# Values of one head pair beside the scores of the next in TensorE's order, the values' sum in another PSUM bank, and the third unit's raw keys asked for later

## The chip, the cores and the metric

One Trainium2 chip, one of its cores. The metric is device time in microseconds (us) of one launch. The kernel before takes 630.86 us (median of three runs, 630.76 to 632.21). A core has TensorE (PE in the rows; its weight loads are PEld), VectorE (DVE), ScalarE (ACT), GpSimd (POOL), SyncE (SP, here only a queue that issues DMAs), and 16 DMA engines. Each engine takes its instructions strictly in the order in which the program lists them.

## What is computed

Two stages, in fp32 accuracy. q, k, v are (4 batches, 8 heads, 768 tokens, 64).

```python
k_sum = k.reshape(B, H, 24, 32, D).max(axis=3)          # 24 summary keys
v_sum = v.reshape(B, H, 24, 32, D).mean(axis=3)
scores = concat(where(|i-j| < 16, q k^T / 8, -1e9), q k_sum^T / 8 + log(32))
a = exp(scores - max); a = a / (sum(a) + 1e-9)
attn = a @ concat(v, v_sum)                              # heads side by side: x is (3072, 512)
h = x @ w_in                                             # 512 -> 2048
g = where(h >= 1, h, where(h <= -1, 0, (h + 1)**2 / 4))
out = g @ w_out                                          # 2048 -> 512
```

## The kernel before

The 3072 tokens are cut into seven units, numbered c = 0 to 6 (`BLOCKS`, line 41): four of 384 tokens, three of 512. The change's own words count them from one, so its "unit 3" is c = 2. Within a unit attention runs by head pairs p = 0 to 3, two heads side by side on 128 partitions. While TensorE does the feed-forward of unit c, the attention of unit c + 1 is put between its matmuls, a pair at a time.

Everything is placed by hand. Two long texts, `OPENING` (line 49) and `REST` (line 72), list the steps of the whole program in one order; `do` (line 740) runs through them, and each engine's instruction stream is this order restricted to that engine. A step is a letter and its arguments in hexadecimal: `s21` is the scores of unit 2, pair 1. The letters that matter here:

- `s` (`scores_of_pair`): 24 matmuls (32 in the wide units) of 64 rows by 64 columns, into two PSUM banks `s_ps`. Then `n` (mask, DVE, two instructions, which empty those banks), `i` (row maxima, DVE), `g` (exponentials, ACT), `h` (reciprocals, DVE), `l` (normalising, POOL), `t` (transposes in blocks, DVE, 10 or 12 a pair) into the one tile `turned_blocks`, and `p`.
- `p` (`values_of_pair`, line 553): 24 or 32 matmuls of 128 rows by 64 columns, which multiply `turned_blocks` with the values into one PSUM bank `o_ps`. `X` (ACT, for the wide units ACT or DVE in turn) and for the narrow units `L` (DVE) bring it to SBUF.
- `F` (`ff1`, three matmuls of 384 columns, line 571; four such steps make one `h`), `G H I` (the gate, on ACT, ACT and DVE), `J O` (its high and low parts, ACT and POOL), `B` (`ff2`, line 695: nine matmuls for a narrow unit). From unit 4 the first product is done by seven half products `1` (line 594) with combinations `9`, and the second is `(`, three matmuls a step.
- `r` asks SP for a pair's raw keys, `R` takes their block maxima (DVE, line 352), `C` copies these beside the window keys (POOL, line 357). `y` asks for raw values, `v` for windowed values, `q` and `k` for queries and window keys, `w` fetches weights, `&` writes weight sets back, `o` stores results: all are DMAs on SP's one queue, in the order of the text, and one that waits for its buffer holds up those behind it.

After the opening, PSUM's eight banks are three pools: `ps_h` (two banks: `h`, half products), `ps_acc` (four banks: `acc`, three or four of them held through a unit's whole second product) and `ps_att` (two banks: `s_ps`, `o_ps` and some half products). As the two `s_ps` need both banks of `ps_att` and `o_ps` needs one, `s` of a pair stands in the order somewhat behind `p` of the pair ahead of it, with some `F` or `B` between.

In SBUF, the tag `"v"` of the pool `load` has two buffers, which windowed values of units 0 and 1 share with the raw keys and raw values of all units from 2 on (lines 131, 163, 169). In the opening the raw keys `r20` and `r21` are asked for between the windowed values `v10`, `v11`, `v13`, `v12` of unit 1, and `R20`, `R21`, `C200` stand near the opening's end. The weights come as raw words, which ACT (lines 237, 243), DVE (250, 255) and POOL (265, 269) turn into two fp32r halves during the opening; `w` steps 14 and 15 are the last two fetches.

Of the kernel before, what the change touches and what calls it, by code (L numbers as in the profile page):

```python
# [74 lines left out]
l201 l200 H16 o01 &10 o02 z21 B12 %001 %000 J13 O13 G14 I16 t202 t20a %014 t205 y22 r22 F150 H14 t209 %002 t207 t200
t206 F151 v20 &61 B13 C210 %015 I14 t208 F170 F171 F152 J16 %016 J14 x200 %017 F153 %003 t204 t20b t203 t201 %004 O14
O16 G15 p20 H15 X20 &05 q22 %005 R22 %006 L20 u22 I15 B14 &01 s21 J15 F172 %007 n211 v21 n210 y23 &02 r23 F173 G17
%101 F180 F181 i21 H17 I17 &51 &11 &03 %100 k22 q23 &04 F182 %102 g213 %103 z22 g212 g211 g215 g214 g210 F183 O15 %104
G18 h21 H18 F190 I18 %105 u23 l210 l211 F191 x210 t216 F192 t215 F193 B15 t219 t21b t214 t210 t212 t211 t217 F1a0 F1a1
J17 F1a2 B16 F1a3 %106 O17 %107 t213 G19 &12 t218 %110 H19 J18 t21a B17 O18 p21 %111 I19 &13 %112 G1a H1a &50 I1a %113  # L80
F1c0 F1c1 X21 C220 L21 F1c2 %114 s22 %115 F1b0 F1b1 %116 n220 n221 %200 i22 J19 %117 %201 g224 F1b2 g223 g225 g220 B18
O19 F1c3 R23 J1a O1a %202 z23 g222 F1b3 g221 %203 h22 G1c %204 H1c G1b I1c v22 &15 k23 l220 l221 H1b %205 B19 I1b %206
F1d0 x220 %207 J1b F1d1 F1d2 F1d3 F1f0 F1f1 O1b t220 t228 t224 t223 G1d F1f2 &14 H1d t222 t225 t221 t22b t227 B1a %210
C230 t229 t22a %211 t226 p22 J1c X22 I1d F1e0 y40 &20 &23 %212 O1c %213 F1e1 L22 F1e2 %214 %215 s23 %301 n231 n230 i23
F1e3 %216 F1f3 G1e B1b %300 H1e g234 g231 v23 &22 g233 J1d I1e %302 F200 %217 g232 %303 &24 k30 g230 O1d %304 g235
F201 G1f H1f %305 x230 F202 h23 B1c %306 J1e &25 &31 l231 l230 I1f %307 O1e t233 t235 t230 t234 F210 %311 q30 %310
F211 &33 B1d J1f B1e t23a t23b t232 t236 t239 t238 t231 O1f t237 p23 X23 u40 %312 %313 L23 B1f F203 C300 U10 G20 s30
F212 %314 H20 %315 o10 %316 n301 F213 G21 I20 J20 n300 H21 F230 F231 F232 i30 g302 g301 I21 %317 r40 k31 v30 &35 J21
g300 U11 g303 g305 g304 O20 F233 F220 G23 F221 F222 F223 O21 G22 H23 B20 o11 h30 l301 l300 x300 C310 H22 I23 %401 I22
t300 t30a F240 F250 F241 F251 F242 t309 t306 t30b %400 t307 t301 t302 &32 t308 U12 J22 B21 t304 t303 t305 J23 p30 F243  # L90
X30 %402 O22 F252 %403 G24 %404 q31 r41 L30 H24 %405 &34 F253 O23 q40 G25 %406 s31 I24 %407 B22 F260 o12 H25 n310 n311
i31 %411 %410 g311 g315 J24 g314 g313 F261 R41 I25 F262 g312 g310 O24 F263 %412 F270 F271 F272 %413 v31 q32 &42 G26
h31 F273 B23 %414 l310 l311 x310 H26 I26 %415 %416 %417 F280 t316 t314 &43 k32 J26 F281 O26 F282 t31b F283 B24 t31a
t313 G27 H27 J25 t311 t312 t319 t310 t317 t315 t318 %501 %500 I27 &71 &45 y41 p31 %502 X31 %503 L31 F290 O25 C320 G28
%504 %505 F291 H28 F292 %506 s32 B25 J27 n320 n321 i32 F293 %510 %507 g324 I28 g321 g320 g322 g323 g325 O27 B26 v32
&44 %511 u41 R40 F2a0 %512 &52 F2a1 h32 J28 G29 k33 x320 &53 q33 F2a2 %513 l320 l321 H29 %514 I29 %515 F2a3 B27 F2b0
O28 %516 F2b1 G2a J29 H2a F2b2 %517 t32b O29 %600 F2b3 %601 t32a C330 t325 t323 t324 t328 t322 B28 t326 G2b t320 t329
t327 t321 p32 I2a y43 &70 &60 &54 %602 H2b I2b &55 F2d0 J2a X32 F2d1 %603 F2c0 L32 s33 %604 F2c1 %605 %610 %611 n330
n331 %606 %607 O2a i33 F2c2 u43 %612 F2c3 F2d2 F2d3 B29 B2a g331 g334 g335 g330 g333 g332 G2c %613 h33 l331 H2c l330
# [722 lines left out]
```

## Time and profile before

| | |
|---|---|
| median of three runs | 630.86 us |
| profiled execution, its own time | 630.26 us |
| its span, first to last instruction | 628.5 us |
| TensorE busy | 609.4 us, 97% |
| DVE, POOL, ACT busy | 437.9, 393.7, 365.0 us |
| mean rate of DMA | 195 GB/s |

The 1.76 us between span and time lie around the instructions. TensorE's busy time counts modelled ends of pipelined matmuls; how much time a group of matmuls takes is better read from the chain of work that ended last, where each piece lasts until the next begins. In a timeline, the bracket behind a row is the idle time of that engine before it, and what ended it.

### The profile page before, as it was taken

What the parts mean: (1) busy time and instruction counts of PE and PEld (TensorE: products, weight loads), DVE (VectorE), ACT (ScalarE), POOL (GpSimd) and SP (SyncE); (2) the same over time, 40 slices, a digit from 0 to 9 for tenths busy, and PEclk for the clock granted to TensorE, in tenths of its full rate; (3) what the DMA queues carried; (4) which work ended last, traced back from release to release, by engine and by line L of the source; (5) the groups of instructions that cost most, each with busy time, mean ns of one, the idle gap of its engine ahead of it and who ended that gap; (6) DMA issues with size and microseconds to landing.
All of it is one profiled execution on the core that took longest, in us unless ns stands there. A gap on an engine that the chain in (4) does not pass through costs nothing.

```text
span 628.5 us, 12987 instructions
## 1 busy us (share of the span) xinstructions
PE 609.4 (97%) x4628; PEld 535.5 (85%) x4628; DVE 437.9 (70%) x1012; ACT 365.0 (58%) x977; POOL 393.7 (63%) x450
## 2 busy tenths in 40 slices
PE   8689998999999999999999999999999999999996
PEld 7578887788888888898888988879988898989895
DVE  5879785568887789778676788865777765444342
ACT  2779997456454655565465665537556365553542
POOL 2578997655676677663477865669674568735421
PEclk9879999999999999999999999999999999999998
DMA  8989835476554667355678497767696485676521
GB/s 305 329 238 382 269 100 142 140 275 202 155 157 159 171 169 216 103 141 133 178 216 270 116 304 231 196 197 217 184 302 175 124 269 146 175 225 186 172 64 67
DMA packets 85041, 122.56 MB, mean 195 GB/s; under 512 B 27377, under 2 KB 56305, under 8 KB 84977
## 3 DMA queue, kind: packets, MB, share of 16 engines
q1 hardware_dynamic: 71152, 77.68, 40.6%
q0 software_dynamic: 13824, 44.05, 23.9%
q8 instruction: 37, 0.61, 0.4%
q14 instruction: 28, 0.22, 0.1%
HBM read 100.73 MB, written 20.97 MB: 194 GB/s over the span
## 4 chain that ended last, share of the span: by engine, by line
PE 89%; DVE 3%; DMA 2%; ACT 2%; POOL 2%; issue 2%; SPq 0%; POOLq 0%; ACTq 0%; DVEq 0%
PE acc L695 41%; PE h L571 20%; PE h L594 19%; PE o_ps L559 3%; PE s_ps L510 3%; DMA halves<-sets 1%; PE o_ps L449 1%; PE t_ps L437 1%; DMA first<-in_kT 1%; PE s_ps L403 1%; ACT raw L237 1%; DVE den L416 1%; PE h_idle L650 0%; DVE vs L361 0%; DVE e L410 0%
## 5 line engine op out<-in xcount | busy, mean ns | idle before, releaser
L695 PE MATMUL acc<-halves,ghi 128*128 128x512 f32 x720 | 224.2, 393 | 0.0
L682 POOL TENSOR_TENSOR glo<-t,ghi 128x384 fp32r<-128x384 f32 (+1 forms) x112 | 126.9, 1135 | 108.6 <-ACT ghi L677 98.9
L695 PEld LDWEIGHTS acc<-halves,ghi 128*128 128x128 f32 x720 | 135.5, 188 | 24.5
L571 PE MATMUL h<-x,halves 128*128 128x384 f32 x720 | 140.5, 342 | 3.1 <-POOL halves L269 2.2
L695 PE MATMUL acc<-halves,glo 128*128 128x512 f32 x360 | 143.0, 397 | 0.0
L594 PEld LDWEIGHTS h<-halves,halves 128*128 128x128 f32 x1008 | 132.4, 190 | 9.6 <-issue 1.8
L664 ACT ACTIVATE t<-h,ones_half 128x256 f32<-128x256 f32 (+1 forms) x160 | 80.2, 513 | 101.0 <-DVE h L607 56.7
L594 PE MATMUL h<-halves,halves 128*128 128x256 f32 x1008 | 135.7, 283 | 1.0 <-DMA halves<-sets 1.0
L571 PEld LDWEIGHTS h<-x,halves 128*128 128x128 f32 x720 | 125.1, 188 | 11.1 <-POOL halves L269 3.1
L672 DVE SCALAR_TENSOR_TENSOR t<-h,t 128x256 f32<-128x256 f32 (+1 forms) x160 | 73.6, 472 | 48.4 <-ACT t L668 44.2
L550 DVE STREAM_TRANSPOSE turned_blocks<-e 32x256 f32<-32x256 f32 (+1 forms) x240 | 98.4, 410 | 5.8 <-POOL e L538 1.8
L677 ACT CAST ghi<-t 128x384 fp32r<-128x384 f32 (+1 forms) x112 | 61.9, 556 | 60.3 <-PE acc L695 38.6
L695 PEld LDWEIGHTS acc<-halves,glo 128*128 128x128 f32 x360 | 67.8, 188 | 12.0 <-issue 1.3
L580 POOL DMA_DIRECT2D halves<-sets x96 | 53.1, 556 | 31.8 <-PE h L594 30.6
L668 ACT ACTIVATE t<-t 128x256 f32<-128x256 f32 (+1 forms) x160 | 71.0, 458 | 2.9
L528 ACT ACTIVATE e<-e,den 128x120 f32<-128x120 f32 x144 | 55.0, 383 | 18.6 <-DVE den L524 18.4
L607 DVE TENSOR_TENSOR sums_so_far<-h,sums_so_far 128x256 f32<-128x256 f32 x72 | 29.5, 421 | 34.2 <-PE h L594 29.0
L607 DVE TENSOR_TENSOR h<-h,sums_so_far 128x256 f32<-128x256 f32 x96 | 39.0, 426 | 20.2 <-PE h L594 18.8
L538 POOL TENSOR_TENSOR e<-e,den 128x480 f32<-128x480 f32 (+1 forms) x40 | 35.6, 910 | 26.3 <-DVE den L533 12.1
L269 POOL TENSOR_TENSOR halves<-w,halves 128x1024 fp32r<-128x1024 f32 x15 | 36.1, 2409 | 5.7 <-DMA q<-in_q 4.2
L517 DVE SCALAR_TENSOR_TENSOR e<-s_ps,mask_sb 128x480 f32<-128x480 f32 (+1 forms) x40 | 22.8, 602 | 14.0 <-PE s_ps L510 14.0
L630 POOL TENSOR_TENSOR merged<-merged,high_of_sums 128x512 fp32r<-128x512 f32 x16 | 20.7, 1296 | 17.8 <-ACT high_of_sums L628 17.6
(115 smaller groups left out, 688.7 us busy)
## 6 DMA issues: line engine op xcount, KB each, us to landing
halves<-sets POOLq DMA_DIRECT2D x72, 512.0 KB, 4.8
raw<-in_w_in SPq DMA_DIRECT2D x15, 512.0 KB, 10.3
raw<-in_w_out SPq DMA_DIRECT2D x15, 512.0 KB, 9.6
v<-in_vwin SPq DMA_DIRECT2D x22, 288.0 KB, 4.0
out<-o SPq DMA_DIRECT2D x24, 256.0 KB, 3.8
halves<-sets POOLq DMA_DIRECT2D x24, 256.0 KB, 4.3
kraw<-in_kT SPq DMA_DIRECT2D x13, 384.0 KB, 4.3
vraw<-in_vT SPq DMA_DIRECT2D x13, 384.0 KB, 4.3
```

The source lines that it names most:

```text
L528: nc.scalar.activation(out=e, in_=e, func=AF.Exp, bias=dens[c, p][:, 0, u:u + 1], scale=1.0, accum_out=dens[c, p][:, 1, u:u + 1])
L550: nc.vector.transpose(out=turned_blocks[kb * SB:(kb + 1) * SB, :2 * nt, qb * SB:(qb + 1) * SB], in_=e[qb * SB:(qb + 1) * SB, :, at:at + SB])
L571: nc.tensor.matmul(hs[c, f][:, :w], weight["win", f][:, part, k * P:(k + 1) * P], x, start=(k == 0 and n == 0), stop=(k == NK - 1 and n == 2))
L580: nc.gpsimd.dma_start(out=at[:, 0] if n == 3 else at.rearrange("p h n -> p (h n)"), in_=cols)
L594: nc.tensor.matmul(hs[c, q, n][:, :HALF], weights[:, wp, kk], x[:, xp, kk], start=(kk == 0 and m == 0), stop=(kk == 1 and m == 2))
L607: nc.vector.tensor_tensor(out=of if to is None else so_far[:, to], in0=of, in1=so_far[:, so], op=ALU.add)
L664: nc.scalar.activation(out=t, in_=h, func=AF.Relu, bias=ones_half, scale=0.5)
L668: nc.scalar.square(out=t, in_=t)
L672: nc.vector.scalar_tensor_tensor(out=t, in0=h, scalar=1.0, in1=t, op0=ALU.max, op1=ALU.min)
L677: nc.scalar.copy(out=hi, in_=ts[c, f])
L682: nc.gpsimd.tensor_tensor(out=lo, in0=ts[c, f], in1=hi.bitcast(F32), op=ALU.subtract)
L695: nc.tensor.matmul(acc[c, i], a[:, rows], weight["wout", f][:, part], start=(f == first and n == 0), stop=(f == last and n == 2))
```

## The change

One line of code moves `o_ps` out of `ps_att`: into `ps_acc` for units 2 to 4, into `ps_h` for units 5 and 6.

```diff
     def values_of_pair(c, p):
         nt = WIDTH[c] // P
-        o_pss[c, p] = ps_att.tile([P, 512], F32, tag="att", name=f"o_ps{c}_{p}")
+        where, tag = (ps_acc, "ps") if c <= CLASSIC else (ps_h, "h")
+        o_pss[c, p] = where.tile([P, 512], F32, tag=tag, name=f"o_ps{c}_{p}")
```

The order of the opening loses five steps (`r20`, `r21`, `R20`, `R21`, `C200`) and is otherwise the same; the order of the rest is written anew, with these five at its head and `y20`, `y21` behind `r20`, `r21`. Of the many lines these are the ones that the prediction speaks of:

```diff
 OPENING = """
...
-c83 F081 I06 F082 F083 bb1 J07 r20 bb0 F0a0 O07 v11 J06 F0a1 ab q13 F0a2 F0a3 c82 E110 cb0 O06 cb2 cb1 d8 E111 e8 cb3
+c83 F081 I06 F082 F083 bb1 J07 bb0 F0a0 O07 v11 J06 F0a1 ab q13 F0a2 F0a3 c82 E110 cb0 O06 cb2 cb1 d8 E111 e8 cb3 D111
...
-P120 N131 T130 A12 X12 I0f T131 P131 L12 F100 J0f P130 B0d O0e R21 ef O0f A13 X13 F112 L13 C200 F101 F102 F113 F103
...
+T130 A12 X12 I0f T131 P131 L12 F100 J0f P130 B0d O0e ef O0f A13 X13 F112 L13 F101 F102 F113 F103 B0e G11 G10 H10 H11
...
 REST = """
-y21 U01 U00 U02 F130 y20 &41 &30 k21 &21 &40 o00 %011 s20 F131 &00 u20 G12 %010 F132 F133 n201 H12 I12 n200 G13 F140
+&50 &40 U02 F130 U00 r20 r21 F131 G12 F132 H12 R20 y20 R21 C200 U01 y21 o01 I12 s20 F160 F133 n200 %011 F161 %010 F162
...
+&20 t230 x230 t232 t231 J1f t234 &33 t23b B1e t23a t235 L22 O1f B1f %310 %311 C300 %312 p23 X23 s30 %313 U10 %314 %315
+L23 F202 n300 F203 %316 G20 F210 n301 i30 H20 %317 g300 F211 F212 k31 o10 I20 g304 F213 G21 H21 g303 g302 J20 I21 g305
...
+1413 I401 H420 9412 I420 9414 (413 (412 U31 9415 {430 {422 p50 J40 s51 O40 X50 n511 G431 n510 1416 9417 i51 (411 (402
```

TensorE's attention steps in their order, before and after; a plus joins two with no other matmul between:

```
before: s20 p20 s21 p21 s22 p22 s23 p23 s30 p30 s31 p31 s32 p32 s33 p33 s40 p40 s41 p41
        s42 s43 p42 p43 s50 p50 s51 s52 p51 p52 s53 p53 s60 p60 s61 p61 s62 p62 s63 p63
after:  s20 s21+p20 s22+p21 s23+p22 p23+s30 s31+p30 s32+p31 s33+p32 s40+p33 s41+p40 s42+p41
        s43+p42 p43+s50 p50+s51 s52+p51 p52+s53 p53+s60 s61+p60 p61+s62 s63+p62 p63
```

## Rows read from the trace of the kernel before

**Rows 1.** Busy time by stage: window, engines' busy us, clock, DMA share, GB/s.
```profile
98.00:119.00 21.00, 17.97 (x133) 15.38 (x132) 11.52 (x24) 12.46 (x30) 15.27 (x17) 1.00 0.45 122
119.00:345.00 226.00, 225.94 (x1674) 196.96 (x1671) 172.94 (x395) 124.23 (x343) 138.86 (x163) 1.00 0.62 184
345.00:613.00 268.00, 267.04 (x2041) 238.31 (x2040) 172.96 (x423) 147.40 (x412) 167.29 (x200) 1.00 0.66 193
```

**Rows 2.** Chain that ended last, separate visits: start us, us, what.
```profile
128.72 0.78 PE s_ps L510 x24
...
158.73 1.58 PE h L571 x9
160.31 2.08 PE acc L695 x9
...
164.99 0.85 PE o_ps L559 x24
165.84 1.79 PE h L571 x9
167.63 0.78 PE s_ps L510 x24
168.41 1.79 PE h L571 x9
...
304.01 0.98 PE s_ps L510 x32
```

**Rows 3.** Chain that ended last, in the opening: scores and values adjacent.
```profile
94.33 0.78 PE s_ps L403 x24
95.11 0.85 PE o_ps L449 x24
95.96 2.28 PE acc L695 x9
```

**Rows 4.** Timeline of TensorE, late opening: its idle times.
```profile
108.44 2.34 PE L571 MATMUL h<-x,halves_win 128*128 128x384 f32 x12 [1.58 <-DVE t L672]
111.66 0.55 PE L437 MATMUL t_ps<-ident_sb,e 128*120 128x128 f32 x3 [0.88 <-DVE w L255]
...
113.83 0.54 PE L437 MATMUL t_ps<-ident_sb,e 128*120 128x128 f32 x3 [0.57 <-POOL e L432]
```

**Rows 5.** Timeline of ACT, late opening: the wait for the last weights.
```profile
103.96 1.15 ACT L237 ACTIVATE raw<-raw 128x1024 f32<-128x1024 f32 x1 [2.93 <-DMA raw<-in_w_out]
```

**Rows 6.** Timeline of SP, the DMA queue, in the opening.
```profile
69.35 1.09 SPq L292 DMA_DIRECT2D kraw<-in_kT  x1
85.00 0.33 SPq L337 DMA_DIRECT2D v<-in_vwin  x1
...
96.05 0.33 SPq L337 DMA_DIRECT2D v<-in_vwin  x1
96.83 1.06 SPq L228 DMA_DIRECT2D raw<-in_w_out  x2
```

**Rows 7.** Timeline of POOL, late opening and behind it.
```profile
105.55 1.29 POOL L269 TENSOR_TENSOR halves_win<-w,halves_win 128x512 fp32r<-128x512 f32 x1
110.24 1.01 POOL L682 TENSOR_TENSOR glo<-t,ghi 128x384 fp32r<-128x384 f32 x1 [3.40 <-ACT ghi L677]
...
112.99 1.54 POOL L432 TENSOR_TENSOR e<-e,den 128x360 f32<-128x360 f32 x2
...
119.89 0.30 POOL L357 COPY k<-ks 128x144 f32<-128x144 f32 x1
...
128.64 0.20 POOL L757 MEMSET sums<- 128x128 f32 x1
```

**Rows 8.** Timeline of DVE, late opening: the block maxima.
```profile
101.35 0.92 DVE L352 TENSOR_REDUCE ks<-kraw 128x24 f32<-128x768 f32 x1
```

**Rows 9.** Groups by line: the copies that empty a wide o_ps.
```profile
L457 DVE COPY xraw<-o_ps 128x512 f32<-128x512 f32 x6 | 4.1, 690 | 5.5 <-PE o_ps L559 5.5
...
L457 ACT COPY xraw<-o_ps 128x512 f32<-128x512 f32 x6 | 3.5, 580 | 5.9 <-PE o_ps L559 5.9
```

More of the change, by code (lines that the diff above doesn't have):

```diff
@@ new lines @@
+G08 B06 N111 H08 db I08 aa S12 W10 M121 ba1 M120 J08 ba0 G0a we f121 ca1 B07 eb F090 F091 ca0 F092 F093 ca3 H0a ca2
+D110 A10 E121 O08 T111 I0a da ac P111 v13 bc1 B08 G09 X10 cc1 F0c0 ea bc0 H09 cc3 F0c1 ad I09 J09 J0a N110 wf cc0 f120
+bd0 F0c2 F0b0 O09 cc2 dc F0b1 bd1 cd0 O0a cd2 C13 F0b2 L10 cd1 F0c3 W11 F0b3 B09 T110 E120 D121 cd3 G0c G0b P110 H0b
+S13 A11 dd H0c B0a ec M130 I0b q21 ed I0c F0d0 D120 k20 ae F0d1 F0e0 F0e1 J0c F0e2 v12 F0d2 M131 J0b f130 be0 f131 ce0
+N120 O0c be1 E130 ce2 O0b af D130 F0d3 X11 N121 ce1 F0e3 ce3 B0b L11 E131 G0d H0d I0d B0c bf1 de ee cf1 bf0 G0e H0e
@@ L75 @@
[L75 to L99, printed above, removed]
@@ L120 @@
-p50 I401 {423 R51 H420 I420 9414 C511 X50 (413 1416 J40 9417 9415 s51 O40 n510 G421 (412 U31 1415 n511 9416 (411 G431
-H421 G430 H431 {430 {433 {432 x510 (400 (401 1424 k52 {431 v52 o32 i51 C520 H430 I431 I430 I421 g512 g516 g510 1422
-R52 1423 9421 J43 g514 1425 9424 9422 g517 g511 9426 g515 g513 9425 h51 (402 1426 O43 z51 (403 1421 G450 H450 G451
-H451 J42 l511 l510 I450 I451 9423 9427 t519 t518 t511 t515 t510 t513 t51a t516 O42 {443 x511 G440 H440 G441 (432 (430
-(431 (433 1430 I440 J45 q53 o31 t512 t514 t517 9430 H441 O45 t51b (422 y53 C521 {442 {440 (421 (420 (423 1432 9431
@@ new lines @@
+F163 B10 n201 k21 i20 B11 u20 G13 g205 g201 g203 H13 g202 u21 %012 J12 I13 %013 O12 g204 g200 F140 F141 %014 J13 h20
+G16 F142 F143 %015 B12 H16 z20 l201 l200 %016 &10 o00 t207 t200 t202 I16 O13 F170 J16 %017 o02 y22 &01 O16 %001 %000
+&04 v20 G14 F171 F172 t208 H14 u22 t206 I14 t204 F173 t20b t203 %002 t201 B13 J14 G17 &05 q22 t209 t20a F150 F151 %003
+C210 t205 F152 F153 s21 O14 x200 %004 %005 H17 I17 G15 p20 n211 n210 F180 H15 &31 r23 %101 %006 i21 F181 k22 B14 I15
+X20 %007 g213 g211 %100 g210 g215 J15 g212 g214 %102 z21 F182 F183 F190 O15 F191 %103 &02 R23 G18 H18 F192 h21 F193
@@ new lines @@
+F230 F231 U11 F232 O20 &35 y43 F233 F220 F221 F222 J21 g301 O21 G23 F223 h30 H23 G22 l301 l300 I23 H22 B20 I22 U12 &11
+&32 o11 v30 J22 O22 t304 t301 F240 F241 F250 F251 C310 F252 F253 F242 F243 B21 t302 t300 t307 t303 t305 t309 t306 t30b
+t30a G25 J23 H25 t308 %400 %401 %402 %403 %404 %405 x300 O23 s31 %406 G24 p30 B22 n311 n310 i31 H24 I25 I24 &34 o12
+&61 %410 %407 %411 g310 g313 F260 g315 %412 %413 J24 g311 g314 F270 F261 F271 F272 %414 F262 k32 g312 v31 h31 O24 F273
+F263 R41 %415 %416 l311 l310 t315 B23 C320 %417 t31b G26 X30 H26 J25 t317 &43 q32 t312 t319 I26 t310 t311 t316 t31a
@@ new lines @@
+t313 t314 &71 B24 %500 t318 &45 F280 F281 %501 O25 J26 G27 H27 x310 %502 F282 O26 F283 L30 s32 %503 G28 p31 n320 n321
+i32 B25 I27 F290 H28 %504 F291 I28 F292 F293 F2a0 F2a1 %505 g324 g323 J27 %510 %511 g322 &42 r40 g325 %506 q33 k33
+F2a2 g320 v32 &44 O27 g321 G29 X31 F2a3 &52 %507 R40 %512 H29 &53 h32 %513 %514 B26 %515 I29 F2b0 l320 F2b1 l321 %516
+&54 J28 t32a F2b2 t324 t322 t327 L31 t321 t329 x320 t325 C330 O28 G2a t326 H2a I2a t320 t323 t328 F2b3 B27 F2d0 J29
+%517 %601 %600 F2d1 F2d2 %602 O29 &55 y41 t32b G2b F2d3 %603 s33 p32 %604 %605 v33 k40 H2b %606 %607 %611 n331 I2b
@@ new lines @@
+n330 B28 i33 F2c0 g330 g335 z40 %610 &63 q41 &62 g333 g334 g332 J2a F2c1 u41 F2c2 B29 X32 O2a g331 J2b G2d F2c3 O2b
+h33 %612 B2a H2d I2d l331 C400 F2e0 l330 %700 %701 x330 G2c L32 %613 F2e1 H2c I2c F2e2 J2c q40 F2f0 F2f1 F2e3 t331
+t333 F2f2 F2f3 B2b t339 O2c G2e H2e t335 J2d t33b t330 %614 t336 t334 r42 &60 t33a %702 t338 t332 %615 t337 %703 %704
+O2d B2c s40 I2e %705 p33 G2f n401 n400 F310 i40 J2e %706 X33 %616 F311 %707 H2f g404 %617 F312 B2d O2e g405 I2f F300
+g401 g400 g402 g406 u43 L33 g403 J2f g407 F313 F301 O2f F302 h40 R42 G31 l401 l400 H31 F303 G30 B2e I31 F320 H30 &64
@@ new lines @@
+k41 F321 I30 F330 t402 F322 &65 v40 t40b t406 t407 t40a t409 t405 t408 t401 t403 t400 F323 F331 F332 B2f J31 x400 F333
+r43 J30 C410 t404 O31 O30 &73 y42 G32 H32 U20 G33 U21 s41 o21 q43 H33 I32 p40 n410 n411 %711 %710 F340 I33 i41 X40
+g416 g415 g413 g411 g414 z41 u42 F341 F342 F343 F350 %712 F351 B30 g417 g410 F352 J32 g412 F353 B31 O32 G34 h41 R43
+%713 l411 l410 o20 H34 B32 &72 k42 v41 y50 J33 I34 J34 q42 O33 F360 F361 G35 F362 H35 U22 t41b t415 t410 B33 t418 x410
+t414 C420 t416 t417 I35 %714 t413 t412 t41a F370 J35 F371 F372 O34 F363 t419 F373 O35 r50 t411 s42 p41 G36 H36 %715
@@ new lines @@
+F3d1 F3d2 I3c t435 t436 t43b F3d3 G3d F3e0 H3d t439 B3a t437 J3c F3e1 {412 x430 C501 t438 t431 t430 t433 t434 O3c t43a
+t432 F3e2 X42 F3e3 B3b I3d p43 &75 x500 s50 G3e {413 H3e J3d F3f0 I3e X43 O3d n501 ^41 z50 n500 F3f1 <41 q51 r51 ^42
+F3f2 1400 F3f3 B3c >41 i50 1401 <44 <42 9400 G3f g502 g500 H3f >42 v51 k51 J3e g503 g504 g507 g501 I3f u51 >44 O3e
+C510 1403 1402 {420 9401 1404 ^43 9403 B3d g505 G400 g506 R51 h50 <45 H400 9402 I400 9404 l501 l500 1410 J3f <46 1411
+B3e >45 9410 O3f 9405 t505 t503 t50b G411 1412 t507 9413 t501 1405 9406 t500 9411 H411 G410 H410 I411 B3f I410 >46
@@ new lines @@
+t515 t510 t512 t51a t516 C521 {443 O45 x511 t519 9430 (423 v52 (421 x520 {440 t517 t511 t51b I440 t518 t514 (452 1432
+9431 s52 I441 n521 n520 J44 p51 i52 1434 1433 g520 g526 g521 g524 1431 g523 g527 g522 q53 k53 9432 1435 X51 g525 9433
+9434 9436 z52 G460 9435 h52 O44 (442 (453 {451 {441 l520 l521 (451 1436 G470 G471 H471 (450 (443 (441 9437 H470 H460
+I471 I470 (440 I460 1441 1440 t528 t52b t521 t525 t529 J47 G461 9440 1444 t527 {452 v53 t526 t520 r53 H461 O47 (471
+1442 (472 I461 t522 t523 t524 9441 9443 9442 t52a (473 (470 1443 J46 G480 H480 x530 {450 x521 O46 C530 R53 {453 (463
@@ new lines @@
+p52 I480 9444 X52 u53 {460 C531 {463 s53 1446 (460 9445 n531 G491 H491 1445 9447 (462 G481 ^50 {462 {461 n530 H481
+I491 9446 G490 I481 1450 (461 1452 i53 J48 9450 H490 v60 k60 I490 1453 9451 z53 1454 g536 g530 9454 9452 1456 O48 1455
+9455 9457 J49 g531 9456 O49 g533 q60 g537 {471 g534 g532 g535 (493 1451 (492 (490 (483 (491 G4b1 (481 (482 h53 9453
+G4b0 G4a1 H4b1 (480 H4a1 I4b1 1460 H4b0 I4a1 I4b0 G4a0 J4b l531 l530 {470 x531 o30 t536 1463 t539 t537 t533 t530 1464
+t53a 9460 t535 1462 t538 t534 t531 t532 t53b O4b C600 {472 {473 x600 {503 H4a0 (4b0 (4b2 9461 p53 I4a0 9464 9462 s60
@@ new lines @@
+9465 X53 n600 n601 J4a G4d1 (4b3 1470 H4d1 <50 1465 O4a 9466 I4d1 G4d0 1461 ^51 ^52 9463 (4b1 H4d0 1466 i60 I4d0 9470
+G4c0 H4c0 9467 J4d (4a3 1472 1471 g606 G4c1 v61 o31 q61 9471 <51 I4c0 (4a1 (4a0 g605 1474 (4a2 1473 <52 H4c1 g603 <54
+g600 I4c1 9474 9472 k61 {501 J4c {500 >50 {502 O4d {510 >51 ^53 O4c (4d3 (4d2 1475 (4d1 (4c2 1476 9475 9473 g607 g601
+g602 9476 g604 h60 <53 G4e0 G4f1 9477 G4f0 H4f1 (4d0 (4c0 I4f1 H4f0 G4e1 H4e1 H4e0 >52 l601 l600 1500 I4e1 9500 <56
+(4c3 1502 t609 I4e0 I4f0 9501 t606 <55 >54 1504 (4c1 t607 9502 J4e J4f t605 >53 >55 t602 O4f 1503 {511 1510 1505 9504
@@ new lines @@
+t603 9506 {512 9505 t604 1501 G510 (4f0 H510 G511 C610 {513 O4e (4f2 I510 t60b t600 H511 (4f3 1511 (4f1 t608 >56 9503
+I511 (4e1 9510 (4e3 U41 J51 G500 1506 (4e2 (4e0 H500 9513 t60a O51 I500 9507 1512 (510 G501 G520 {520 {521 {522 H501
+H520 t601 I501 1514 9511 I520 9512 1513 9514 s61 9515 n610 n611 U40 o41 J50 i61 O50 x610 U42 G531 p60 (512 (513 H531
+X60 g612 (503 g614 g617 o40 {523 I531 q62 U43 {533 (500 1516 1515 1520 g610 g611 g613 g616 g615 9516 9517 9520 G521
+G530 (511 H530 1521 h61 1522 H521 (502 9523 I530 9521 I521 J53 l611 l610 t617 t610 q63 (501 1526 1524 1523 O53 k62
@@ new lines @@
+{530 v62 t614 t618 9522 t615 (530 o42 o43 (532 (531 G540 t61a {542 J52 t619 t612 9524 9527 1525 {531 O52 (520 (533
+(522 (521 C620 {540 {532 t613 9526 (523 G541 H541 G550 H550 t61b 9525 t611 t616 H540 G551 I541 I540 I550 H551 p61 s62
+k63 J54 I551 X61 1533 1530 J55 n620 n621 O55 9530 (550 1534 1531 1532 i62 O54 {543 {541 {553 9531 9533 g621 g620 (553
+9532 g623 g627 9534 (551 1536 g625 g622 9535 1535 9537 G560 g624 g626 G571 h62 H571 9536 H560 G570 G561 l620 {551 H561
+l621 H570 I571 I560 I561 (543 (541 t62b I570 t626 t62a (552 t628 t622 t620 t623 1540 (540 (542 v63 1541 9540 J57 J56
@@ new lines @@
+1543 C630 O57 O56 1542 {550 1544 (570 (572 9541 9544 t621 {552 9543 t627 9542 t625 9545 1546 (573 (560 (562 (571 G580
+H580 {562 ^60 I580 {563 x620 (563 (561 {560 9547 t629 t624 G591 H591 G581 s63 H581 I581 p62 n631 I591 n630 1545 X62
+J58 9546 i63 1550 G590 1552 9550 H590 1554 9551 I590 9552 1553 1551 g633 J59 1556 1555 O58 {561 O59 9553 9554 9555
+9556 g637 g630 g631 g635 g632 (591 (593 (590 g634 9557 G5b1 G5b0 g636 H5b0 G5a0 I5b0 {572 {573 G5a1 h63 H5a0 H5b1 {570
+{571 x630 H5a1 l631 l630 I5b1 (580 (592 (581 I5a0 (582 I5a1 1560 1562 9560 J5a (583 t633 t639 1564 J5b 1563 t636 9561
@@ new lines @@
+t634 t63a 9562 1565 1566 O5b t63b 9564 9565 9566 t630 G5d1 9567 t631 G5d0 H5d1 {602 O5a I5d1 H5d0 G5c1 (5b2 1561 I5d0
+(5b1 t635 H5c1 (5b0 (5a2 1573 I5c1 t632 9563 (5b3 1570 (5a0 {600 {601 {603 t637 <63 G5c0 H5c0 t638 {613 >63 J5d O5d
+9570 (5a1 p63 (5d2 (5d0 (5a3 X63 I5c0 <60 (5d3 1572 9571 1574 1575 9572 9574 >60 ^62 J5c <62 9576 1576 G5f0 ^61 1571
+O5c 9575 9577 H5f0 (5d1 {611 {612 {610 >62 (5c1 (5c3 G5f1 I5f0 9573 <61 G5e1 H5f1 G5e0 H5e1 I5f1 I5e1 J5f H5e0 >61
+(5c0 1600 (5c2 O5f 1603 I5e0 9600 J5e 1602 O5e <64 ^63 (5f1 (5f2 (5f0 1601 <66 (5e1 (5f3 9601 9603 >64 G600 1604 H600
@@ new lines @@
+J64 {641 {640 O64 9630 1636 (652 9631 (650 (653 1633 9632 (640 1631 9634 9637 9633 {652 9635 (642 (651 1635 G661 9636
+H661 G660 H660 G671 H671 G670 I661 H670 I660 I671 I670 J66 (641 (643 1640 1642 9640 9641 1646 1644 1643 1645 9642 9646
+9644 J67 9647 9645 {653 {650 {651 O66 O67 G681 G691 H691 (673 (670 (672 G690 H681 o52 o53 (663 (671 1641 I681 {660
+9643 I691 {661 {662 H690 G680 I690 (661 (662 (660 1650 J69 9650 H680 1653 1654 O69 I680 (692 1652 9651 (690 1655 9652
+9654 9655 9656 {663 J68 G6b1 G6b0 H6b1 H6b0 (691 1651 (693 1656 I6b1 I6b0 9653 9657 1660 J6b O68 {673 9660 G6a1 {670
@@ new lines @@
+(682 O6b {672 H6a1 (683 G6a0 H6a0 (681 I6a0 I6a1 (680 1664 (6b2 (6b0 1662 (6b1 1663 9661 9664 J6a 9662 9665 G6d1 (6b3
+O6a H6d1 {671 I6d1 (6a3 1665 1666 (6a1 1661 (6a0 9667 9666 9663 G6d0 (6a2 H6d0 I6d0 G6c1 1670 1674 J6d H6c1 9670 G6c0
+I6c1 1672 9671 9672 H6c0 O6d 1673 9674 I6c0 (6d1 1675 9675 (6d3 1676 J6c G6f1 1671 (6d2 (6d0 O6c 9676 G6f0 H6f1 H6f0
+I6f1 9677 9673 G6e1 I6f0 G6e0 J6f H6e0 (6c2 H6e1 O6f (6c0 (6c3 (6c1 (6f0 I6e1 I6e0 J6e O6e (6f1 (6f3 (6f2 (6e2 (6e0
+(6e1 (6e3 U62 U60 U61 U63 o62 o63 o61 o60
```

101 lines of the change are left out of this document (24 added, 77 removed).

## The prediction

> **What bounds the kernel now.** First the busy time by stage [rows 1]. From 119 to 345 us TensorE is busy 225.94 of 226 us, from 345 to 613 us 267.04 of 268: there TensorE is the bound, no other engine comes near, and a change pays only by what it takes from TensorE's own instruction stream. From 98 to 119 us, late in the opening, 3.03 of 21 us are idle: there something else is the bound. So I read two things: in the chain what a visit to the attention costs TensorE, and in the timelines of the late opening who makes it wait.
>
> *A visit.* In the chain nine `h` matmuls take 1.58 us when they follow the feed-forward's own work and 1.79 behind `o_ps`, and again 1.79 behind `s_ps` [rows 2]. So coming back from a visit costs 0.21 us beyond the visit's own 0.85 or 0.78. (The chain books it on the piece behind; I use it only as a price per visit.) The opening holds one place where `s_ps` and `o_ps` of two pairs stand side by side: they take 0.78 and 0.85 as when apart, and the nine `acc` matmuls behind take 2.28 [rows 3] against 2.08 undisturbed [rows 2]. Two visits in one thus pay one return of 0.20, not two.
>
> *The late opening.* TensorE stands idle 1.58, 0.88 and 0.57 us, together the 3.03 [rows 4]. The first two hang on ACT by way of DVE (gate, weight conversion), the third on POOL, whose `glo` had waited 3.40 us for ACT [rows 7]. ACT itself stood for 2.93 us until the last weights landed, at 103.96 [rows 5]. They came late because SP asked for them at 96.83, and SP was late because the windowed values ahead on its queue found no buffer: the raw keys `r20` took one of the two `"v"` buffers at 69.35, so `v11` waited until 85.00 and `v13` until 96.05, with the weights behind [rows 6].
>
> **The change, part by part.**
>
> *Joints.* The new order joins 19 pairs of visits and leaves two single; before, none of 40 was joined. 19 x 0.20 = 3.8 us less, all of it on TensorE's stream where that is the bound [rows 1]. Thirteen joints are scores and then values, as in rows 3. Six are values and then scores, which no row shows: at best they save half as much again (0.3 us, an estimate from that 0.20), at worst they cost another 0.2, if the two shapes disturb each other. I take 0.20, the value of the nearest row; the bounds put the term between -4.4 and -1.4.
>
> A joint goes from tiles of 64 x 64 to tiles of 128 x 64. Rows 3 show that this leaves the pieces at 0.78 and 0.85, and one return of 0.20 behind. The Trainium skill, TensorEngine Tiling (Array Packing), section Tiling Modes, Key Properties, says that a change of tiling mode, not only of tile, drains the TensorE; read strictly, a joint pays a drain of its own. If that cost as much as a return, the 3.8 would vanish; by the row the run-out of the scores is within their 0.78 already, joined or not, and the saving stands. The measurement decides here.
>
> *The opening's DMAs.* Without `r20`, `v11` takes the free buffer at about 69.4, `v13` takes the one that `v11` gets now, at 85.00, and the last weights follow as they now follow `v13`, 0.78 behind: about 85.8 in place of 96.83. From that issue they took some 6 to 7 us to ACT; they lie there by 93, and ACT wants them at 101.03. Its 2.93 us go. Then: the first idle time (1.58) waits for a gate that comes 2.93 earlier; what is late next is `halves_win`, which POOL ends at 105.55 + 1.29 = 106.84 [rows 7], and TensorE was ready at 108.44 - 1.58 = 106.86, so nothing is left of it. The second (0.88) hangs on ACT's conversions, 2.93 earlier against 2.46 wanted: gone. The third wants 3.03 and POOL's chain gains at most 2.93: 0.1 stays. `R20`, 0.92 us of DVE in the midst of it [rows 8], goes too and helps the conversions. So up to 2.9; the ends are 0 (another wait stands right behind) and 3.03 (all the idle time). I take 2.5, near the upper end as each step of it has its row, less something for waits under these that no row shows.
>
> *What moves behind the opening.* `R20`, `R21` and `r20`, `r21`, `y20`, `y21` are now late, not gone. DVE has room: 172.94 us in 226. `C200` goes on POOL from 119.89 to behind the memset that ends at 128.64 + 0.20, so `s20` can have its keys at 128.84 + 0.30 = 129.14 at the earliest [rows 7]. It starts now at 128.72 and stands two `F` steps later in the new order, 2 x 0.53 (a third of 1.58), at 129.8 [rows 2]: 0.6 us of room. All of this shifts together with the opening. I cost it at 0; if `R21` or a `y` holds DVE or SP, up to 0.9 (one block maximum).
>
> *Time to work.* Counted in `F` (0.53), `B` (2.08) and visits, TensorE's work between scores and values of a pair was at least 12.2 us in the order before and is at least 14.4 now: DVE, ACT and POOL get more time for a pair, not less. At the units' ends it is tighter: `F203` needs `X23` and `L23`, at most 0.58 + 0.69 (the wide copies, rows 9, as a bound for the narrow), and has `s30` and `F202` in front, 0.78 + 0.53 = 1.31. Zero, with 0.2 a boundary as the other end.
>
> *The banks.* In units 2 to 4 `acc` holds three of four banks and `o_ps` the fourth: nobody waits. In units 5 and 6 `o_ps` holds one of the two `h` banks until `X` is done. At `p50`, `s51` stands between it and the next half product: 0.98 [rows 2], and `X` takes 0.58 or 0.69 [rows 9]. I cost it at 0, with 0.7 (one gate instruction or copy ahead of `X`) for each of eight visits as the other end. The 0.96 us idle from 345 to 613 I leave as it is.
>
> *Sum.* 630.26 (the profiled execution: span 628.5 and 1.76 around it) - 3.8 - 2.5 = 623.96. The median of the runs shown lies 0.6 above that execution; I say 624.3.
>
> **The rivals.**
>
> *The opening gives nothing back* (0.20). The idle time only changes its owner: POOL, 15.27 busy of 21 [rows 1], has conversions, `glo` and `e` in one line. Against it: POOL itself idles 3.40 us for ACT in this stretch. 630.26 - 3.8 = 626.5.
>
> *The joints save nothing* (0.07): the change of shape costs what the return cost. Rows 3 speak against, for thirteen of the nineteen. 630.26 - 2.5 = 627.8. This is the result that the strict reading of the Trainium skill's TensorEngine Tiling (Array Packing), Key Properties, would give.
>
> *New waits eat it* (0.08): four unit boundaries, `s20` and the eight visits that hold an `h` bank wait 0.4 each, 13 x 0.4 = 5.2 us together: 623.96 + 5.2 = 629.2. No row shows such a wait; the whole order is new, which speaks for some.
>
> *Slower: the feed-forward loses its second bank* (0.05). In units 5 and 6 each `p` holds one of two `h` banks, and behind it on DVE or ACT stand a gate instruction or a copy and `X` itself, 0.69 + 0.69; where nothing covers them, 1.4 us a visit. Eight visits: 11.2, so 635.2. It makes the kernel slower from (6.3 + 1.9) / 8 = 1.0 us a visit on. Against it: `s` or other work stands behind each. The Trainium skill, TensorEngine Tiling (Array Packing), PSUM Bottleneck, warns that tiling speeds up the TensorE but not the emptying of PSUM; that is this mechanism.
>
> **How the numbers follow.** Forecast 0.60, 622.5 to 625.8; the rivals as above. About 0.3% (1.9 us) is what a measurement of this kernel can tell from no change. Faster by more: forecast, first two rivals, most of 0.60 + 0.20 + 0.07 = 0.86; within: 0.09; slower: 0.05. The range: below, all joints at their best and all idle time of the opening, 630.26 - 4.4 - 3.0 = 622.9, and the 0.96 us, 621.9; above it holds the first two rivals, 628.0.
>
> **What would show it.** Right: joined visits with one 0.2 behind; no ACT wait for `in_w_out` near 101; the last weights asked for near 86; the piece after the opening some 2.5 us earlier; TensorE idle under 1 us from 119 on. Wrong: a new bracket at `s20`, at `F203` and its like, or before half products behind `p5` and `p6`; or a PE wait for POOL at 106 to 114 as long as before.

## The result, and the profile after

| | before | after |
|---|---|---|
| median of six runs, us | 630.81 (629.08 to 632.21) | 621.72 (620.93 to 623.92) |
| profiled execution, us | 630.26 | 620.93 |
| its span, us | 628.5 | 619.2 |
| mean granted clock of TensorE in it | 0.989 | 0.996 |

The ratio is 0.9865, with a 95% interval of 0.9843 to 0.9887: 9.1 us less where 6.6 were forecast (630.86 to 624.3). The median lies 0.2 below the low end of the range, 621.9; the clock, below, put it there.

First the stages of the profile after; the columns are those of [rows 1], and the last stage ends ten us earlier, as the kernel is that much shorter.

```profile
98.00:119.00 21.00, 20.49 (x148) 18.07 (x147) 10.74 (x23) 13.53 (x33) 14.63 (x15) 1.00 0.24 85
119.00:345.00 226.00, 225.07 (x1694) 199.65 (x1693) 180.68 (x409) 127.48 (x360) 145.33 (x170) 1.00 0.64 184
345.00:603.00 258.00, 258.00 (x1989) 231.35 (x1988) 169.04 (x408) 140.72 (x389) 160.18 (x192) 1.00 0.67 196
```

The late opening has 0.51 us of idle TensorE left of 3.03. From 119 on 0.93 us are idle in all, against 0.06 + 0.96 before [rows 1], and none at all from 345.

The late opening went by the steps of the prediction. SP's timeline after, from the step that asked for `r20` before:

```profile
69.68 1.19 SPq L337 DMA_DIRECT2D v<-in_vwin  x1
...
83.45 0.33 SPq L337 DMA_DIRECT2D v<-in_vwin  x1
83.83 0.91 SPq L228 DMA_DIRECT2D raw<-in_w_out  x2
...
110.71 4.23 SPq L292 DMA_DIRECT2D kraw<-in_kT  x2
```

`v11` goes at 69.68 and `v13` at 83.45, the last weights at 83.83 in place of 96.83 [rows 6]. On ACT the weights' first step, with a bracket of 2.93 before [rows 5], has none:

```profile
99.35 1.14 ACT L237 ACTIVATE raw<-raw 128x1024 f32<-128x1024 f32 x1
```

TensorE's timeline, with the three places of [rows 4] and the two waits that stand after 119:

```profile
105.02 2.34 PE L572 MATMUL h<-x,halves_win 128*128 128x384 f32 x12
107.19 0.49 PE L437 MATMUL t_ps<-ident_sb,e 128*120 128x128 f32 x3
...
109.24 0.55 PE L437 MATMUL t_ps<-ident_sb,e 128*120 128x128 f32 x3 [0.51 <-POOL e L432]
...
145.30 1.31 PE L572 MATMUL h<-x,halves 128*128 128x384 f32 x6 [0.28 <-DVE t L673]
...
181.18 0.81 PE L572 MATMUL h<-x,halves_win 128*128 128x384 f32 x3 [0.65 <-DVE t L673]
```

1.58 and 0.88 are gone. The third stays, 0.51 of 0.57: it waits for POOL, whose row in between waited for ACT 1.22 us in place of 3.40 [rows 7] and was then busy without a break:

```profile
105.63 1.02 POOL L683 TENSOR_TENSOR glo<-t,ghi 128x384 fp32r<-128x384 f32 x1 [1.22 <-ACT ghi L678]
106.72 1.60 POOL L391 COPY v<-mean 24x768 f32<-24x768 f32 x2
108.39 1.54 POOL L432 TENSOR_TENSOR e<-e,den 128x360 f32<-128x360 f32 x2
...
124.21 0.30 POOL L357 COPY k<-ks 128x144 f32<-128x144 f32 x1
```

The last row is `C200`; `s20` follows at 125.18 with no wait. In the chain (start us, us, what) it stands first here, and below it a joint of each kind:

```profile
125.18 0.78 PE s_ps L510 x24
...
210.63 0.78 PE s_ps L510 x24
211.41 0.85 PE o_ps L560 x24
212.26 2.27 PE acc L696 x9
...
331.37 1.08 PE o_ps L560 x32
332.45 0.98 PE s_ps L510 x32
333.44 0.72 PE h L572 x3
```

Scores and then values take 0.78 and 0.85, and the nine `acc` behind 2.27 against 2.08 undisturbed: what [rows 3] showed of the opening's joint (0.78, 0.85, 2.28). Values and then scores, which no row of before showed, leave the scores at 0.98, as alone [rows 2], with one return behind: three `h` matmuls take 0.72, where a third of the undisturbed 1.58 is 0.53.

**Part of the difference is TensorE's clock in the first 40 us, not the change.** One stretch of both profiles (columns as above, the clock is third from the end), before and then after:

```profile
31.40:38.20 6.80, 5.54 (x50) 4.52 (x45) 4.94 (x11) 4.19 (x12) 4.13 (x6) 0.50 1.00 306
```

```profile
31.40:38.20 6.80, 4.94 (x79) 3.98 (x75) 6.73 (x16) 6.04 (x15) 4.19 (x6) 1.00 1.07 320
```

Before, TensorE ran at 1.2 GHz (0.50) there, after at 2.4 (1.00). The order of steps is the same up to that point, and TensorE's 313th matmul, the first behind that stretch of before, starts at 38.22 us before and at 36.57 after. These 1.65 us come ahead of all that was changed. Where TensorE falls to the lower level differs between launches of one kernel: the mean clock of the runs of before lies between 0.986 and 0.997, of after between 0.987 and 0.996, and a run takes some 0.35 us more per 0.001 less (0.39 and 0.32 by a straight line through each kernel's runs). Read from these lines at a clock of 0.992, before (58 runs) stands at 630.0 and after (12 runs, with the repetition below) at 622.1. So the change itself is worth 7.9 us. The two profiles say 7.7: from the 313th matmul to TensorE's last one 584.90 us before, 577.22 after; the profile of the repetition has 577.46 there, which would make it 7.4. Taken from 630.86, 7.4 to 7.9 us lead to 623.0 to 623.5, inside the range.

### The profile page after: what moved, and what is told of

The parts are those of the page before. It is cut to its first block, busy times and chain, and to the rows that moved or that the text cites. A ratio compares the mean times of both kernels' runs of the same rounds, so it can differ in the third digit from the quotient of the medians.

```text
span 619.2 us, 12970 instructions
## 1 busy us (share of the span) xinstructions
PE 603.1 (97%) x4628; PEld 535.2 (86%) x4628; DVE 441.4 (71%) x1012; ACT 364.6 (59%) x977; POOL 394.5 (64%) x450
## 4 chain that ended last, share of the span: by engine, by line
PE 87%; DVE 3%; DMA 3%; POOL 2%; ACT 2%; issue 1%; SPq 0%; POOLq 0%; ACTq 0%; DVEq 0%
PE acc L696 41%; PE h L595 20%; PE h L572 19%; PE o_ps L560 3%; PE s_ps L510 3%; DMA raw<-in_w_in 2%; DVE turned_blocks L550 1%; DVE merged L625 1%; PE o_ps L449 1%; DMA first<-in_kT 1%; POOL e L432 1%; PE t_ps L437 1%; POOL halves L269 1%; ACT raw L237 1%; PE s_ps L403 1%
## 5 line engine op out<-in xcount | busy, mean ns | idle before, releaser
L572 PE MATMUL h<-x,halves 128*128 128x384 f32 x720 | 138.0, 339 | 3.0 <-POOL halves L269 1.8
L625 DVE TENSOR_TENSOR merged<-merged 128x128 f32<-128x128 f32 x64 | 28.6, 447 | 2.0 <-POOL merged L622 0.7
```

Source lines behind the costliest of these rows:

```text
L572: nc.tensor.matmul(hs[c, f][:, :w], weight["win", f][:, part, k * P:(k + 1) * P], x, start=(k == 0 and n == 0), stop=(k == NK - 1 and n == 2))
```

## The experiments

All stand beside runs of the kernel before on the same chip. "At 0.992" is the value of the line of time against granted clock; where a kernel's clock didn't spread around that value there is none. The rows come from three chips: the first four from one, "mostly first visit ahead" and the rows "once more", "one sum later" and "both of these" from a second, "17 joints" and "more idle products" from a third. The kernel before stands there at 629.8, 630.0 and 630.5 at 0.992, so rows of different chips compare to about half a microsecond.

| kernel | median us (range, runs) | ratio to before, 95% | at 0.992 |
|---|---|---|---|
| opening alone | 628.81 (628.33 to 630.0, 12) | 0.9978, 0.9967 to 0.9990 | 628.9 |
| rest alone | 625.58 (625.0 to 626.58, 6) | 0.9927, 0.9910 to 0.9943 | 625.4 |
| before, `r20` behind the weights | 627.35 (625.03 to 631.25, 12) | 0.9960, 0.9940 to 0.9981 | 627.6 |
| after, joints undone, second visit later | 632.23 (630.52 to 633.03, 12) | 1.0020, 1.0006 to 1.0033 | 632.3 |
| after, joints undone, mostly first visit ahead | 631.07 (629.5 to 633.66, 12) | 1.0012, 0.9991 to 1.0033 | 631.6 |
| after, 17 joints undone where it costs no wait | 626.13 (624.49 to 626.7, 7) | 0.9925, 0.9896 to 0.9953 | 626.0 |
| after, once more | 622.20 (621.57 to 622.87, 6) | 0.9867, 0.9836 to 0.9899 | 622.1 |
| after, one sum later | 621.82 (621.43 to 622.44, 4) | 0.9860, 0.9825 to 0.9895 | 621.9 |
| after, more idle products in the opening | 621.88 (620.84 to 622.08, 6) | 0.9856, 0.9827 to 0.9885 | |
| after, both of these | 620.19 (619.93 to 620.57, 5) | 0.9834, 0.9803 to 0.9865 | |

### The opening's part alone

```diff
 OPENING: r20 r21 R20 R21 C200 left out
-y21 U01 U00 U02 F130 ...
+r20 r21 R20 R21 y21 U01 U00 U02 C200 F130 ...
```

> The kernel before with only the opening's part: r20, r21, R20, R21, C200 stand at the head of the rest, o_ps stays in its bank, no visit is joined. My theory (the DMA queue set the late opening): ACT no longer waits near 101 us for the last weights, TensorE's idle time in the late opening falls from 3.0 us to about 0.5, s20 may wait 0.3 for C200; about 2.5 us less than before (628.3). Rival, the joints or the new order bring all: within 0.5 us of before (630.8). Rival, the opening brings more than its idle time (4.5 us, as the raw difference of the two profiles would have it): 626.3.

It brought 1.75 us (1.1 at equal clock), less than the 2.5 expected. The late opening and the stage behind, and two rows of TensorE's timeline:

```profile
98.00:119.00 21.00, 20.52 (x149) 18.22 (x148) 11.83 (x25) 13.00 (x32) 17.09 (x17) 1.00 0.18 52
119.00:345.00 226.00, 224.43 (x1659) 194.92 (x1658) 174.05 (x395) 123.71 (x342) 137.78 (x162) 1.00 0.62 185
```

```profile
127.01 0.85 PE L510 MATMUL s_ps<-k,q 64*64 64x120 f32 x24 [0.42 <-POOL k L357]
...
130.62 0.62 PE L571 MATMUL h<-x,halves 128*128 128x384 f32 x2 [0.97 <-DVE t L672]
```

The idle time of the late opening falls to 0.48, as in the whole change, but 1.57 us of idle time stand behind it, where before had 0.06: in the old order `s20` follows `F130` so soon that it waits for `C200`, and an `h` waits for DVE, which has the sum of the first raw values (`u20`) ahead of that gate:

```profile
128.50 0.95 DVE L367 TENSOR_REDUCE sums<-vraw 128x24 f32<-128x768 f32 x1 [3.99 <-DMA vraw<-in_vT]
129.49 0.18 DVE L368 TENSOR_SCALAR sums<-sums 128x24 f32<-128x24 f32 x1
129.57 0.53 DVE L517 SCALAR_TENSOR_TENSOR e<-s_ps,mask_sb 128x360 f32<-128x360 f32 x1
130.02 0.55 DVE L672 SCALAR_TENSOR_TENSOR t<-h,t 128x384 f32<-128x384 f32 x1
```

The raw values are asked for behind the raw keys on the same queue, so they are late now too, and DVE stands 3.99 us for them with masks and gate behind. The new order has `s20` two steps later and `u20` further back. The five steps and the order of the rest belong together.

### The rest alone

```diff
 OPENING: r20 r21 R20 R21 C200 at their old places
-&50 &40 U02 F130 U00 r20 r21 F131 G12 F132 H12 R20 y20 R21 C200 U01 ...
+&50 &40 U02 F130 U00 F131 G12 F132 H12 y20 U01 ...
```

> The changed kernel with the opening of the kernel before (the five steps back in their places). My theory (19 joints at 0.20): 3.8 us less than before, and about 1 more or less by single waits that come or go: 626 to 627.5. Rival, the opening is most of it: within 1.5 us of before. If the two parts are independent, the gains of this run and of the opening alone add up to that of the change.

```profile
98.00:119.00 21.00, 17.94 (x133) 15.34 (x132) 11.93 (x23) 12.51 (x31) 15.25 (x17) 1.00 0.45 125
...
345.00:600.00 255.00, 255.00 (x1967) 228.52 (x1966) 168.79 (x408) 139.19 (x387) 161.96 (x194) 1.00 0.69 203
```

The 3.06 us of idle time stay, and 5.0 us go (4.6 at equal clock): the joints and what the new order does beside them. This and the part above add up to 6.75 (5.7 at equal clock) of the whole change's 9.1 (7.9). Of the 2.2 that are missing at equal clock, 1.5 is the idle time that the old order lets in behind the opening, above; for the other 0.7 no row was found.

### Only `r20`'s request behind the last weights

```diff
-F083 bb1 J07 r20 bb0 F0a0 ...
+F083 bb1 J07 bb0 F0a0 ...
-N110 wf cc0 ...
+N110 wf r20 cc0 ...
```

> The kernel before with one request moved: r20 stands behind the last weight fetch on the DMA queue; R20, r21, R21 and C200 stay in the opening. My theory (the queue, not the work of DVE): ACT's 2.9 us wait for the last weights goes, late-opening idle time falls from 3.0 to under 1 us, time 2 to 2.9 us less than before, as with the whole opening part. Rival, it is R20 in DVE's line that costs: no change from before.

One request moved, `R20`, `R21` and `C200` where they were. SP's and ACT's timelines:

```profile
70.66 1.12 SPq L337 DMA_DIRECT2D v<-in_vwin  x1
...
86.99 0.33 SPq L337 DMA_DIRECT2D v<-in_vwin  x1
87.36 0.91 SPq L228 DMA_DIRECT2D raw<-in_w_out  x2
98.46 0.33 SPq L292 DMA_DIRECT2D kraw<-in_kT  x1
```

```profile
102.93 1.14 ACT L237 ACTIVATE raw<-raw 128x1024 f32<-128x1024 f32 x1
```

ACT doesn't wait, and TensorE is busy 20.79 of the 21 us, more than with the whole change. So the queue alone made the idle time; DVE's work for `R20` in this stretch cost TensorE nothing. The time falls by 3.2 us (2.4 at equal clock). The profiled run, at 631.25 the slowest of the twelve, gains 3.0 at the same places and loses 1.5 of it near 415 us, where a half product waits 2.5 us for its weight set. That wait was 1.0 in the profile of before and 0.4 in that of the opening alone; whether the change or the launch made it longer stays open.

### The joints undone, two ways

Both keep the opening and the order of the rest, and set one step of the feed-forward between the two visits of each of the 19 joints: the first kernel puts the second visit one step later, the second kernel the first visit one step ahead (in 16, where what it needs allows; the second one later in 3).

```diff
-F152 F153 s21 O14 ... H17 I17 G15 p20 n211 n210 F180 H15
+F152 F153 s21 O14 ... H17 I17 G15 n211 n210 F180 p20 H15
```

> The changed kernel with its 19 joints undone and nothing else: the second visit of each joint stands one feed-forward step later (for s51 its masks too), same banks, same opening. My theory: each of the 19 pays a return again, 0.20 us, 3.8 in all: 625.5. Rival, the new order of the other engines brings the gain and the joints nothing: 621.7, the same as the changed kernel. Rival, only the thirteen scores-then-values joints save and the six others do not: 2.6 more, 624.3.

```diff
-F152 F153 s21 O14 ... H17 I17 G15 p20 n211 n210 F180 H15
+F152 s21 F153 O14 ... H17 I17 G15 p20 n211 n210 F180 H15
```

> The joints undone a second time, without the waits of the first try: in sixteen of the nineteen the first visit stands one feed-forward step earlier, in three the second one later. My theory: 19 returns of 0.20 come back, 3.8 us over the changed kernel, with under 1 us of idle TensorE beside them: about 626.5 if the changed kernel is at 622. Rival, the joints matter by covering waits, not by their returns (the first try lost 10): 6 us or more over it, as idle time in the trace. Rival, joints worth nothing: the same as the changed kernel.

They cost 10.2 and 9.4 us over after at equal clock, where 19 returns are 3.8: both expectations failed. What TensorE waited for from 119 to 600 us (total us, times, longest) in the first:

```profile
PE h L572 <- DVE t L673: 3.1, 4, 1.1
PE h L595 <- DVE e L517: 1.6, 2, 0.8
PE h L595 <- ACT xraw L457: 1.4, 2, 0.7
```

and in the second:

```profile
PE h L572 <- DVE t L673: 1.5, 2, 0.8
PE o_ps L560 <- POOL k L357: 1.4, 1, 1.4
PE o_ps L560 <- DVE turned_blocks L550: 1.0, 1, 1.0
```

Two rows of the first kernel's TensorE timeline show how such a wait comes about:

```profile
145.69 0.85 PE L510 MATMUL s_ps<-k,q 64*64 64x120 f32 x24
147.66 0.80 PE L572 MATMUL h<-x,halves 128*128 128x384 f32 x3 [1.13 <-DVE t L673]
```

A new `h` needs the bank of the `h` two before, and gets it when DVE has taken the gate's minimum from it. In the joined order both visits, 1.63 us, lie ahead of that `h`, and 0.28 of waiting is left; with the visits apart only 0.85 lies there, and 1.13 is left. A joint thus also covers the emptying of a bank. In the second kernel, where under 1 us of idle time was expected, 4.03 of 226 are idle from 119 to 345, since visits put ahead come before their blocks or sums are ready. Neither kernel prices a return; the next one does.

### Seventeen joints undone, each in the way that showed no wait

```diff
 as the second kernel above for s21 s22 s31 s32 s33 s40 s42 s43 p50 p52 p53 s63
 as the first for p22 s30 s50 p60 s62; s41+p40 and s52+p51 stay joined
```

> Seventeen of the 19 joints undone, each by that one of the two earlier ways (first visit a step earlier, or second a step later) whose trace showed no wait there; the two that waited in both ways (s41 with p40, s52 with p51) stay joined. My theory, the return of 0.20 us and the cover are two prices: 17 x 0.20 = 3.4 over the changed kernel, and no more than 0.5 us of idle TensorE from 119 us on beside the 0.9 that the changed kernel has; about 625.6 against 622. Rival, a separate visit always brings a wait: 6 us or more over it.

```profile
119.00:345.00 226.00, 225.20 (x1677) 196.63 (x1676) 180.00 (x402) 125.57 (x354) 142.64 (x167) 1.00 0.61 179
345.00:600.00 255.00, 254.78 (x1957) 226.93 (x1956) 167.33 (x405) 138.87 (x385) 160.88 (x193) 1.00 0.69 202
```

TensorE is idle 1.02 us in these stretches against 0.93 of after, so what is left is the returns. The time is 3.9 us above after at equal clock. Between the 313th and the last matmul it is 4.0 against the profile of after and 3.8 against that of its repetition. Less the 0.1 of idle time that is 0.22 to 0.23 for each of 17, where 0.20 was taken.

### After once more, and two edits on top

The same kernel beside the next two, to see what a second set of launches gives:

> The changed kernel once more, as the measure for the three beside it on this chip. If the part of its gain that lies ahead of every changed instruction (1.6 us of half clock in the opening that its profile lacks and that of before has) is chance, more runs put it nearer to 7.7 us under before (about 623) than to 9.1.

Its median of 622.20 lies 7.8 under that of before in the same set, 629.96. That fits the account that the part of the 9.1 that lies ahead of the changed steps was chance.

Then the wait of 0.65 at 181. DVE's timeline of after ahead of it:

```profile
177.12 0.95 DVE L367 TENSOR_REDUCE sums<-vraw 128x24 f32<-128x768 f32 x1
178.10 0.74 DVE L368 TENSOR_SCALAR sums<-sums 128x24 f32<-128x24 f32 x1
178.76 0.96 DVE L517 SCALAR_TENSOR_TENSOR e<-s_ps,mask_sb 128x360 f32<-128x360 f32 x2
179.75 0.90 DVE L524 TENSOR_REDUCE den<-e 128x6 f32<-128x720 f32 x1
180.57 1.01 DVE L673 SCALAR_TENSOR_TENSOR t<-h,t 128x384 f32<-128x384 f32 x2
```

The gate's minimum, in the last row, stands behind the sum of raw values (`u23`, the first two rows), which nobody wants soon. The edit puts `u23` behind that minimum:

```diff
-%207 J1c F1e1 u23 F1e2 ...
+%207 J1c F1e1 F1e2 ...
-H1e I1e I1d F1f0 ...
+H1e I1e I1d u23 F1f0 ...
```

> The changed kernel with u23 (the sum of raw values, 1.1 us of DVE) behind the two gate minima I1e and I1d that TensorE waits for at 180 us. My theory: the one wait left behind the opening (0.8 us before F1f0) goes, and nothing takes its place; 0.8 us less, in the trace, hardly in the median. Rival: the next thing on DVE (n23, i23) makes the same wait: no change.

The wait went, and some 0.3 us with it at equal clock (0.5 between the 313th and the last matmul). The other edit gives TensorE more idle products where it waits in the opening, alone and then with `u23`. Idle products are matmuls on zeros that nobody reads; `j` is such a step. One gets more matmuls, and three are added:

```diff
-E010 c00 j065 T001 ...
+E010 c00 j06d T001 ...
+j0a3 ahead of F000, j0b4 ahead of Z03, j0c2 ahead of T021
```

> The changed kernel with the 16 idle products of the opening alone, u23 in its old place. My theory: the clock stays full in the opening as with both (0.998 to 1.000 in the mean) and nearly all of that version's gain over the changed kernel (about 2 us) is this: 620.2 to 621.0, with the wait of 0.65 us at 180 us back. Rival, the two only work together or u23 brought half: 621.5 or more.

> The same, and 16 more idle products (two matmul records each) in the four gaps of the opening between 18 and 34 us, where TensorE waits. My theory: where the granted clock fell to half near 32 us (it did in five of six profiles and cost the first 38 us up to 2.6 us) it no longer does, the median falls by about 1 us more and the runs spread less: 621 or under. Rival: the clock falls for another reason, or the products delay what waits behind them: no change or up to 1 us slower.

The first 60 us of after, and of the kernel with both:

```profile
0.00:60.00 60.00, 51.28 (x484) 44.63 (x485) 47.33 (x106) 41.49 (x109) 35.57 (x45) 0.97 0.96 309
```

```profile
0.00:60.00 60.00, 54.27 (x521) 47.57 (x522) 48.07 (x108) 42.53 (x111) 36.31 (x46) 1.00 0.98 322
```

The filled kernels keep the clock at 0.995 to 1.000 in all runs, where after had 0.987 to 0.996. Yet the fill alone gained 0.3 at most, and its expectation failed. Its two runs at a clock of 1.000 took 622.07 and 622.08, no less than after; perhaps the products stand in TensorE's way, but no row shows that. With both edits the time is 620.19, 2.0 below after in the same set of launches, and the two ranges don't meet. That is the best version here and beats both kernels. Why both bring more than the sum of each alone stays open: in the profile with both the wait at 181 is gone, but a new one of 0.5, of a half product for DVE, stands behind it.

## Why the prediction was right, and where it was short

*Joints: right, a little small.* Taken at 19 x 0.20 = 3.8; the seventeen undone say 0.22 to 0.23 each, so 4.2 to 4.4 for nineteen. The open point, values and then scores, came out at the value of the nearest row: the scores behind values take 0.98 as alone, and one return follows.

*That the change of shape drains away the gain: refuted.* Pieces of 0.78 and 0.85 side by side, and one return. From the last start of the scores to the first start of what follows, TensorE takes 192 to 193 ns when it returns to 128 x 128 (all 20 visits of before) and 192 to 217 when it goes on to the values (all thirteen joints of after); behind values it is 151 to 152 either way, but for the return at 145.30 with its wait of 0.28. So a joint does pay for its change of shape. It saves because two visits apart change shape four times and a joint three. The Trainium skill, TensorEngine Tiling (Array Packing), section Tiling Modes, Key Properties, says that a change of tiling mode drains the TensorE. The trace agrees in so far as those 192 and 152 ns show behind every group, whatever shape comes next; within a joint they lie in the 0.78 already, and nothing comes on top.

*The opening: right in its mechanism, small in its size.* The sum's term was 2.5, with 3.03 as the upper end; it measured 2.95 where matmuls of the two profiles are set side by side (behind the 313th matmul they are 1.64 earlier at 42 us, and 4.59 from the third place on: 113.83 against 109.24). The idle time itself fell by 2.52, from 3.03 to 0.51: the 0.4 taken off for hidden waits is what the third place kept, 0.51 in place of 0.1. What was small is the price of a wait. The first two places moved by about 1.8 and 1.05 (108.44 against 105.02, 111.66 against 107.19), where their brackets say 1.58 and 0.88. A bracket begins at the modelled end of the matmul ahead, which lies later than the next matmul would start without a wait: from 333.65 us of after, undisturbed `h` matmuls start 173 to 176 ns apart and are booked as 334 to 337 ns each. The requests went within 2.0 us of the forecast (1.65 of it are the clock's), ACT's wait went whole, and the run with only `r20` moved shows the queue as the one cause.

*Costs set at 0.* `s20` had room, and the run with the opening alone shows what its new place is worth: 0.42 and 0.97 in the old one. `F203` and its like, and the units' boundaries, show no wait. The second bank of `h` is never missed: from 345 us on TensorE isn't idle at all. A narrow unit's `o_ps` in a bank of `h` wasn't tried. New waits came elsewhere, 0.28 and 0.65, both of an `h` for DVE's gate minimum. I had counted DVE's time per pair and not what stands ahead of that one instruction.

*Left as it was, and wrong.* The 0.96 idle from 345 to 613 [rows 1] I took over unchanged. It was one wait of a half product for its weight set, and with the new order it is gone; so the new waits cost nothing on balance, 1.02 idle before and 0.93 after.

*The sum.* 2.95 from the opening and 4.2 to 4.4 from the joints make 7.2 to 7.4, idle time 0.1 more; the change is worth 7.4 to 7.9. What remains, 0.6 at most, I can't give to a row. The forecast was 6.3. The other 1.65 of the 9.33 between the profiled executions is the clock of the opening's first 40 us, which the prediction didn't weigh: it set its sum against one execution at a clock of 0.989 and left 0.6 for the way from there to the median.

*The rivals.* The opening gave something back in one form only, that of the old order. New waits did come, a fifth of the 5.2 of that rival.
